# One normalisation of three moved from VectorE to GpSimd, with the steps around it reordered, in a softmax attention and mish feed-forward kernel

## The chip, the cores and the metric

The kernel runs on one core of a Trainium2 chip. The metric is the device time of one execution in microseconds (us); lower is better. Times are medians over several executions; one further execution was taken with the hardware profiler, and every duration below comes from it. Engines are called as the profile calls them: PE is TensorE (PEld its weight loads), DVE is VectorE, ACT is ScalarE, POOL is GpSimd, SP is SyncE, which here only issues DMAs.

## The reference

Attention over 8 batches, 12 heads, 448 positions and head size 64, then a feed-forward layer with mish over the 3584 rows (768 to 2048 to 768):

```python
scores = scale * np.matmul(q, k.transpose(0, 1, 3, 2))
m = np.max(scores, axis=-1, keepdims=True)
e = np.exp(scores - m)
attn = e / (np.sum(e, axis=-1, keepdims=True) + np.exp(-m) + 1e-09)
out = np.matmul(attn, v)
...
h = x @ w_in
g = h * np.tanh(log1p(exp(h)))        # mish
y = g @ w_out
```

## The kernel before

**Pairs and units.** Two heads of one batch form a pair; there are 48 pairs (0 to 47). Six head pairs make a batch. Pairs 0 to 5 are handled one by one in a head loop. From pair 6 on, three pairs form a unit; the loop variable `u` runs from 2 to 17, and units 2 to 15 hold attention (pairs `3u` to `3u+2`, the first of them is `p0`). Units are called u2, u3 and so on here. All instructions of an engine run in the order in which the program writes them (`tc.manual_schedule()`), so the place of a call in this loop is the place of its instructions in the queue of each engine.

**The exp stage of a unit** has twelve steps `n` (four steps for each pair, `s = n % 4`). A step lets ACT take the exponentials of one score tile (`exps`, L282; the row sums come with it), empties late PSUM tiles through DVE (`flush_late`), puts in filler matmuls of the second feed-forward product (`mm2_part`, L428, from u4 on), and issues the next scores on PE (L248 or L254), whose row maxima DVE takes (`negm`, L269). There are three score tiles `sc0` to `sc2`. In the steps with `s == 0` (n = 0, 4 and 8) the unit loads a pair that is four ahead (`load_pair`, three DMAs on SP, L120) and casts a pair that is three ahead to bf16 (`cast_pair`, three casts on POOL, L161 to L163). POOL also issues the weight loads (`load_w`, L147) in u2 to u4.

**The feed-forward stage of a unit** then runs eight steps `f`. Each is one column block of the first product (`mm1_mish`: six matmuls, L373, and one Mish on ACT, L379). At `f == 0` DVE computes the denominators (L295, L299) and normalises the first pair: `normalise` is seven multiplications in place, one for each tile of 128 rows, on `en` (L305), and then one transposing DMA on SP that makes `eT` from `en` (L312). At f = 1, 3 and 5 PE turns q and k of one pair of the next unit (`transpose_pair`, L178, into two banks of `sc2` and `sc1`), DVE copies the turned q out with the scale (`evac_qk`, L209, two instructions; L199 up to pair 11) and ACT copies k (L217). The copies are called q1, q2 and q3 here, the turnings t1, t2 and t3. At f = 1 and 3 the second and the third pair are normalised, behind q1 and q2 in DVE's queue. The score of the next unit's step 0 is issued at f = 3, those of steps 1 and 2 at f = 6 and 7.

**Attention times v** (`av_pair`, L349) of the unit's pairs runs in the exp stage of the unit after it; from u4 on in front of the last score of each pair (`av_with`). u2 and u3 follow the table `AV_AT` instead. Pairs 5, 6 and 7 (`BY_PE`) are not turned by a DMA but by PE (`turn_on_pe`, L323, copied out by DVE, L327); in u3 that is pair 6 at n = 0 (two pieces), 2 and 3, and pair 7 at n = 4 to 7. The exponentials of pairs 10 and 11 reuse the `en` buffers of pairs 6 and 7, so they can start only when these turnings have read them.

Of the kernel before, what the change touches and what calls it, by code (L numbers as in the profile page):

```python
# [9 lines left out]
FP32 = mybir.dt.float32  # L10
BF16 = mybir.dt.bfloat16
AF = mybir.ActivationFunctionType
ALU = mybir.AluOpType
# [6 lines left out]
def kernel(  # L20
# [9 lines left out]
    nc = tc.nc  # L30
# [10 lines left out]
    NTILE = 2 * S // 128  # L41
# [3 lines left out]
    FF_U = FF_T // UNITS_PER_B  # L45
# [17 lines left out]
    st_pool = pool("st", 5)  # L63
# [38 lines left out]
    def flush_late():  # L102
        while late:
            late.popleft()()
# [8 lines left out]
    def load_pair(p):  # L113
        if p >= N_PAIRS:
            return
        b, h0 = p // HP, (p % HP) * 2
        tiles = []
        for nm, src in (("q", q), ("k", k), ("v", v)):
            t = ld_pool.tile([SP_, 2, NT * D], FP32, tag=f"{nm}_f", name=f"{nm}_f")
            nc.sync.dma_start(  # L120
                out=t, in_=src[b, h0 : h0 + 2].rearrange("h (p t) d -> p h (t d)", t=NT)
            )
            tiles.append(t)
        loaded[p] = tiles
# [25 lines left out]
    def cast_pair(p):  # L150
        if p >= N_PAIRS:
            return
        q_f, k_f, v_f = loaded.pop(p)
        q_bf = bf_pool.tile([SP_, NT, 2, D], BF16, tag="q_bf", name="q_bf")
        k_bf = bf_pool.tile([SP_, NT, 2, D], BF16, tag="k_bf", name="k_bf")
        v_bf = bf_pool.tile([SP_, 2, NT * D], BF16, tag="v_bf", name="v_bf", bufs=12)
        by_t = "p h (t d) -> p t h d"
        cast_q, cast_k = nc.gpsimd.tensor_copy, nc.gpsimd.tensor_copy
        if p == 0:
            cast_q, cast_k = nc.vector.tensor_copy, nc.scalar.copy  # L160
        cast_q(out=q_bf, in_=q_f.rearrange(by_t, t=NT))  # L161
        cast_k(out=k_bf, in_=k_f.rearrange(by_t, t=NT))  # L162
        nc.gpsimd.tensor_copy(out=v_bf, in_=v_f)  # L163
        casted[p] = (q_bf, k_bf, v_bf)
# [56 lines left out]
    def scores_ahead(limit):  # L221

        while rg["next"] < limit and rg["used"] < len(sc_tiles):
            rg["used"] += 1
            scores(rg["next"])
            rg["next"] += 1
# [71 lines left out]
        )  # L298
        nc.vector.reciprocal(out=st["rden"], in_=st["den"])  # L299

    def normalise(p, dma=True):
        st = att[p]
        en = st["en"]
        for i in range(NTILE):
            nc.vector.tensor_scalar(  # L305
                out=en[:, :, i, 0:SP_], in0=en[:, :, i, 0:SP_],
                scalar1=st["rden"][:, i : i + 1], scalar2=None, op0=ALU.mult,
            )
        eT = eT_pool.tile([128, NT, 2 * S], BF16, tag="eT", name="eT")
        st["eT"] = eT  # L310
        if dma:
            nc.sync.dma_start_transpose(  # L312
                out=eT.rearrange("c j (i q) -> c (j i) q", q=128),
                in_=en.rearrange("q j i c -> q (j i c)"),
            )
# [19 lines left out]
    def av_pair(p, act=False, bank=None):  # L335
        b, hp = p // HP, p % HP
        eT = att[p]["eT"]
        v_bf = casted[p][2]
        if b not in xT:
            xT[b] = xT_pool.tile([128, DM_T, S], BF16, tag="xT", name="xT")  # L340
        av = mo_take() if bank is None else bank
        for j in range(NT):
            for h in range(2):
                if p >= DIAG_FROM:
                    by_h = eT[0:SP_, j, :].rearrange("c (i h r) -> c h i r", h=2, r=64)
                    e_h = by_h[:, h]
                else:
                    e_h = eT[0:SP_, j, h * S : (h + 1) * S]
                nc.tensor.matmul(  # L349
                    av[h * 64 : (h + 1) * 64, 0:S],  # L350
                    lhsT=v_bf[:, h, j * D : (j + 1) * D],
                    rhs=e_h,
                    start=(j == 0), stop=(j == NT - 1),
                )
        copy = nc.scalar.copy if act else nc.vector.tensor_copy

        def evac():
            copy(out=xT[b][:, hp, :], in_=av[:, 0:S])  # L358
            if bank is None:
                mo_free.append(av)  # L360

        late.append(evac)
        del att[p], casted[p], qkT[p]
# [77 lines left out]
    first_mm2 = 2 * UNITS_PER_B  # L441
# [24 lines left out]
    weight = [5.2] + [1.0] * (steps - STEPS) + [0.4] * (STEPS - 1)  # L466

    LEAD = UNIT_PAIRS + 1
    HEAD = HP

    BY_PE = {HEAD - 1: 1, HEAD: 0, HEAD + 1: STEPS}
    AV_AT = {0: {5: 3, 7: 4, 10: 5}, 1: {5: 6, 10: 7}}

    W_AT = ({5: 1, 9: 1}, {1: 1, 5: 1, 7: 1, 9: 1, 11: 1}, {1: 1, 3: 1, 5: 1, 7: 1})
    for p in range(UNIT_PAIRS):
# [10 lines left out]

    for p in range(HEAD):
        for s in range(STEPS):
# [7 lines left out]
            if s:  # L496
                flush_late()
            scores_ahead(HEAD * STEPS + 3)
            if s == (2 if p == HEAD - 1 else 0):
                load_pair(p + 4)  # L500
# [5 lines left out]
            if s == 1:  # L506
                if p:
                    normalise(p - 1)
            if s == 3 and p + 3 < HEAD + 2:
                transpose_pair(p + 3)  # L510
            if s == 3 and p >= 3:
                av_pair(p - 3, act=True)
    denominators(att[HEAD - 1])
    normalise(HEAD - 1, dma=HEAD - 1 not in BY_PE)

    for u in range(UNITS_PER_B, N_UNITS + 2 * UNITS_PER_B):
        attn = u < N_UNITS
        filler = deque()
        for part in plan.get(u, []):
            filler.extend(mm2_part(*part))  # L520
        total, done, acc = sum(w for _, w in filler), 0, 0.0
        p0 = u * UNIT_PAIRS
        if attn and u >= first_mm2:
            av_with.update({p0 + i: p0 + i - UNIT_PAIRS for i in range(UNIT_PAIRS)})
        end = min((u + 1) * UNIT_PAIRS, N_PAIRS) * STEPS

        for n in range(steps):
            pi, s = divmod(n, STEPS)
            p, idx = p0 + pi, p0 * STEPS + n
            late_tp = u == UNITS_PER_B and n == STEPS  # L530
            if late_tp:
                transpose_pair(p0 + 2)
            exps(idx)
            if late_tp:
                evac_qk(p0 + 2)
            if u == UNITS_PER_B + 1 and n == 0:
                av_pair(p0 - 1)
                for j in range(2):
                    turn_on_pe(HEAD, j)
            flush_late()  # L540
            acc += weight[n]
            want = int(total * acc / sum(weight) + 1e-6)
            while done < want:
                fn, w = filler.popleft()
                fn()
                done += w
            scores_ahead(end)
            if s == 0:
                load_pair(p + LEAD)
                cast_pair(p + LEAD - 1)  # L550
            early = AV_AT.get(u - UNITS_PER_B)
            if early is not None:
                if n in early:
                    av_pair(early[n])
                for pe, n0 in BY_PE.items():
                    first = 2 if pe == HEAD else 0
                    if pe // UNIT_PAIRS == u - 1 and n0 + first <= n < n0 + NT:
                        turn_on_pe(pe, n - n0)
            elif s == (2 if pi else 0) and N_PAIRS <= p < N_PAIRS + UNIT_PAIRS:
                av_pair(p - UNIT_PAIRS)  # L560
            if u - UNITS_PER_B < len(W_AT):
                load_w(W_AT[u - UNITS_PER_B].get(n, 0))
        assert done == total

        moe = u < N_UNITS + UNITS_PER_B
        b, w = (u - UNITS_PER_B) // UNITS_PER_B, u % UNITS_PER_B
        nxt = p0 + UNIT_PAIRS
        todo = sorted(range(p0, nxt), key=lambda p: p in BY_PE)
        for f in range(FF_U):
            if moe:  # L570
                mm1_mish(b, w * FF_U + f)
            if u == UNITS_PER_B and f in (2, 6) or u == UNITS_PER_B + 1 and f == 1:
                load_w(1)
            if not attn:
                continue
            if f == 0:
                denominators(att[p0]["whole"])
                normalise(todo[0], dma=todo[0] not in BY_PE)
            if f == 3:
                scores_ahead(min(nxt * STEPS + 1, N_PAIRS * STEPS))  # L580
            if f in (1, 3, 5):
                transpose_pair(nxt + f // 2, bank=f // 2 % 2)
                evac_qk(nxt + f // 2)
            if f in (1, 3):
                p = todo[(f + 1) // 2]
                normalise(p, dma=p not in BY_PE)
            if f >= FF_U - 2:
                scores_ahead(min(nxt * STEPS + f - FF_U + 4, N_PAIRS * STEPS))
    flush_late()
    assert not pieces and all(have == 4 for _, have in o_sbs.values())  # L590

# [29 lines left out]
```

## Time and profile before

| What | Value |
|---|---|
| Median of 3 runs | 510.11 us (509.66 to 511.9) |
| The profiled execution itself | 506.53 us |
| Its span from first to last instruction | 504.8 us, mean granted PE clock 0.986 |
| Busy in the span | PE 458.0, DVE 373.6, ACT 350.3, POOL 100.9 us |
| `en<-en,rden` on DVE (L305) | 336 instructions, 97.2 us |
| Casts on POOL (L161 to L163) | 142 instructions of about 623 ns |
| `eT<-en` transposing DMA (L312) | 45 issues, median 6.4 us from issue to landing |

The profiled execution took 506.53 us and lies 3.6 us under the median of the runs; 1.7 us of it are outside the span. In the trace's timeline a line gives start, duration, engine, line, operation, output and inputs, the number of instructions merged, and in square brackets the idle time before it and what ended that. The unit boundary used below is the one small exponential at the end of a unit's exp stage (L292): 98.46 us for u3, 126.87 for u4, then 153.74, 182.20, 210.26, 238.18 (u8), 265.97, 293.60, 321.53, 349.10, 376.73, 404.30 and 431.18 (u15).

### The profile page before, as it was taken

How to read it: one execution, taken by the hardware profiler on the slowest of the kernel's cores; microseconds unless marked ns; L12 is line 12 of the kernel's file. 1: busy time of each engine (PE TensorE's matmuls, PEld its weight loads, DVE VectorE, ACT ScalarE, POOL GpSimd, SP SyncE). 2: the span in 40 equal slices, each digit the busy share in tenths (PEclk: the TensorE clock that was granted, in tenths of full speed). 3: DMA queues.
4: the chain of work that ended last, by engine and by line, in shares of the span. 5: the costliest groups of instructions: out<-in, count | busy, mean ns of one | idle time of the engine just before them, and what ended most of it. 6: DMA issues, size and time to landing. Idle time of an engine off the chain costs nothing.

```text
span 504.8 us, 9065 instructions
## 1 busy us (share of the span) xinstructions
PE 458.0 (91%) x3120; PEld 250.5 (50%) x3120; DVE 373.6 (74%) x778; ACT 350.3 (69%) x906; POOL 100.9 (20%) x168
## 2 busy tenths in 40 slices
PE   4466987988999999999999999999999999999996
PEld 2122444544555555455555555555555555555573
DVE  4897997888979797978889797978798897530011
ACT  5988657768797877968696878879697879602300
POOL 4523263405022130402121120404040200000000
PEclk9999987899999999999999999999999999999999
DMA  8999999999998969698998879797989776670122
GB/s 227 189 200 242 250 196 241 197 179 251 153 252 192 188 169 214 199 202 217 188 250 167 192 148 226 200 215 203 203 233 182 184 131 145 120 171 11 53 53 73
DMA packets 209454, 92.21 MB, mean 183 GB/s; under 512 B 166272, under 2 KB 205952, under 8 KB 209408
## 3 DMA queue, kind: packets, MB, share of 16 engines
q1 hardware_dynamic: 201920, 85.35, 77.9%
q0 software_dynamic: 7488, 6.29, 8.5%
q8 instruction: 24, 0.39, 0.3%
q14 instruction: 22, 0.18, 0.1%
HBM read 45.61 MB, written 11.01 MB: 112 GB/s over the span
## 4 chain that ended last, share of the span: by engine, by line
PE 47%; DVE 31%; ACT 12%; DMA 5%; issue 3%; SPq 1%; POOL 0%; DVEq 0%; ACTq 0%; POOLq 0%
PE mo L428 20%; DVE en L305 12%; PE mo L373 11%; ACT en L282 11%; DVE negm L269 11%; PE sc L248 6%; PE sc L349 5%; DVE qd L209 3%; DMA k_f<-in_k_dram 3%; DMA eT<-en 2%; DVE xT L358 2%; PE sc L178 1%; PE mo L349 1%; PE sc L254 1%; PE mo L323 1%
## 5 line engine op out<-in xcount | busy, mean ns | idle before, releaser
L282 ACT ACTIVATE en<-sc,negm 128x448 bf16<-128x448 f32 x336 | 209.2, 636 | 30.5 <-DVE negm L269 15.4
L269 DVE TENSOR_REDUCE negm<-sc 128x2 f32<-128x896 f32 x192 | 181.5, 969 | 44.2 <-PE sc L248 33.3
L428 PE MATMUL mo<-w_out_sb,gT 128*128 128x384 bf16 (+2 forms) x1152 | 167.1, 309 | 0.0
L373 PE MATMUL mo<-xT,w_in_sb 128*128 128x448 bf16 x672 | 141.5, 355 | 0.4 <-DVE xT L358 0.3
L428 PEld LDWEIGHTS <-gT 128*128 128x128 bf16 (+1 forms) x1152 | 97.3, 100 | 56.5 <-issue 5.9
L379 ACT ACTIVATE gT<-mo 128x448 bf16<-128x448 f32 x112 | 59.3, 543 | 74.7 <-PE mo L373 74.5
L373 PEld LDWEIGHTS <-w_in_sb 128*128 128x128 bf16 x768 | 73.2, 98 | 64.4 <-issue 4.4
L305 DVE TENSOR_SCALAR en<-en,rden 128x448 bf16<-128x448 bf16 x336 | 97.2, 361 | 1.4
L161 POOL CAST q_bf<-q_f 112x512 bf16<-112x512 f32 x47 | 29.3, 623 | 282.9 <-DMA q_f<-in_q_dram 245.7
L414 DVE COPY o_sb<-mo 128x384 f32<-128x384 f32 (+1 forms) x64 | 32.1, 501 | 58.3 <-PE mo L428 58.1
L248 PE MATMUL sc<-kT,qd 128*128 128x448 bf16 x252 | 71.7, 354 | 3.6 <-DVE qd L209 2.7
L282 ACT ACTIVATION_READ_ACCUMULATOR en<-sc,negm 128x1 f32 x336 | 69.2, 206 | 0.0
L248 PEld LDWEIGHTS <-qd 128*128 128x128 bf16 x252 | 23.3, 97 | 35.9 <-issue 16.5
L349 PE MATMUL sc<-eT,v_bf 112*64 112x448 bf16 x288 | 34.0, 356 | 2.3 <-ACT en L282 1.8
L254 PE MATMUL sc<-kT,qd 64*128 64x448 bf16 x36 | 17.9, 515 | 18.1 <-ACT en L282 15.2
L349 PEld LDWEIGHTS <-v_bf 112*64 112x64 bf16 x384 | 21.3, 114 | 24.9 <-issue 17.0
L217 ACT COPY kT<-sc 128x448 bf16<-128x448 bf16 x39 | 20.8, 535 | 17.4 <-PE sc L178 17.4
L163 POOL CAST v_bf<-v_f 112x512 bf16<-112x512 f32 x48 | 29.9, 622 | 13.7 <-DMA v_f<-in_v_dram 12.8
L162 POOL CAST k_bf<-k_f 112x512 bf16<-112x512 f32 x47 | 29.3, 623 | 6.3 <-DMA k_f<-in_k_dram 4.5
L209 DVE TENSOR_SCALAR qd<-sc 64x448 bf16<-64x448 bf16 x72 | 27.8, 386 | 0.9
L178 PEld LDWEIGHTS <-q_bf 112*128 112x128 bf16 x192 | 14.4, 104 | 25.3 <-issue 11.8
L358 DVE CAST xT<-sc 128x448 bf16<-128x448 f32 x36 | 22.1, 614 | 0.0
(45 smaller groups left out, 251.3 us busy)
## 6 DMA issues: line engine op xcount, KB each, us to landing
q_f<-in_q_dram SPq DMA_DIRECT2D x48, 224.0 KB, 4.6
k_f<-in_k_dram SPq DMA_DIRECT2D x48, 224.0 KB, 4.8
v_f<-in_v_dram SPq DMA_DIRECT2D x48, 224.0 KB, 4.8
w_in_sb<-in_moe_w_in_dram POOLq DMA_DIRECT2D x12, 256.0 KB, 5.2
w_out_sb<-in_moe_w_out_dram POOLq DMA_DIRECT2D x8, 384.0 KB, 7.8
out_dram<-o_sb SPq DMA_DIRECT2D x7, 336.0 KB, 3.0
out_dram<-o_sb SPq DMA_DIRECT2D x8, 288.0 KB, 3.8
out_dram<-o_sb SPq DMA_DIRECT2D x8, 240.0 KB, 2.8
```

What stands on the lines that cost most here:

```text
L163: nc.gpsimd.tensor_copy(out=v_bf, in_=v_f)
L209: nc.vector.tensor_scalar(out=qd[rows, :, h, :], in0=q_ps[rows, 0:S].rearrange("d (i r) -> d i r", i=QB), scalar1=SCALE, scalar2=None, op0 ...
L248: nc.tensor.matmul(sc[:, bk, 0:S], lhsT=qT[:, i].rearrange("d h r -> d (h r)"), rhs=kT, start=True, stop=True,)
L269: nc.vector.tensor_reduce(out=negm, in_=sc[:, 0 : len(cols), 0:S], axis=AX.X, op=ALU.max, negate=True)
L282: nc.scalar.activation(out=st["en"][:, :, c, 0:SP_], in_=sc[:, bk, 0:S].rearrange("q (j c) -> q j c", j=NT), func=AF.Exp, bias=st["negm"][ ...
L305: nc.vector.tensor_scalar(out=en[:, :, i, 0:SP_], in0=en[:, :, i, 0:SP_], scalar1=st["rden"][:, i : i + 1], scalar2=None, op0=ALU.mult,)
L349: nc.tensor.matmul(av[h * 64 : (h + 1) * 64, 0:S], lhsT=v_bf[:, h, j * D : (j + 1) * D], rhs=e_h, start=(j == 0), stop=(j == NT - 1),)
L358: copy(out=xT[b][:, hp, :], in_=av[:, 0:S])
L373: nc.tensor.matmul(h_ps[:, 0:S], lhsT=w_in_sb[:, dm, ff * 128 : (ff + 1) * 128], rhs=xT[b][:, dm, :], start=(dm == 0), stop=(dm == DM_T - 1),)
L379: nc.scalar.activation(out=gT[b][:, ff, :], in_=h_ps[:, 0:S], func=AF.Mish)
L414: nc.vector.tensor_copy(out=o_sb[:, cols], in_=st["o"][:, 0:n_cols])
L428: nc.tensor.matmul(st["o"][r : r + n, 0:n_cols], lhsT=gT[bb][:, ff, c0 : c0 + n], rhs=w_out_sb[:, ff, cols], start=(ff == 0), stop=(ff == ...
```

## The change

From u4 on, the third pair of a unit is normalised by POOL instead of DVE: seven multiplications in the form with two scalars (the second is 1.0), placed at f = 4. Its reciprocals are first copied on DVE into a tile of their own (`rden2`). The second pair's normalisation moves on DVE from behind q1 (f = 1) to behind q2 (f = 3, after the score that is issued there and its maxima). In u2 and u3 the third one stays on DVE and moves to f = 7, behind the maxima of the scores issued there. Loads and casts come at exp steps n = 0, 3 and 6 (the first, fourth and seventh step) instead of 0, 4 and 8. In u3 the product of pair 8 no longer leads step 0 but comes at n = 3, in front of the turning of that step, and that of pair 6 moves from n = 5 to n = 6. The weight loads keep their steps, so some of them now stand behind a cast that they stood before.

```diff
-    def normalise(p, dma=True):
+    def normalise(p, dma=True, on_pool=False):
         st = att[p]
         en = st["en"]
+        if on_pool:
+            st["rden2"] = st_pool.tile([128, NTILE], FP32, tag="rden2", name="rden2")
+            nc.vector.tensor_copy(out=st["rden2"], in_=st["rden"])
         for i in range(NTILE):
-            nc.vector.tensor_scalar(
+            args = dict(
                 out=en[:, :, i, 0:SP_], in0=en[:, :, i, 0:SP_],
-                scalar1=st["rden"][:, i : i + 1], scalar2=None, op0=ALU.mult,
-            )
+                scalar1=st["rden2" if on_pool else "rden"][:, i : i + 1],
+            )
+            if on_pool:
+                nc.gpsimd.tensor_scalar(scalar2=1.0, op0=ALU.mult, op1=ALU.mult, **args)
+            else:
+                nc.vector.tensor_scalar(scalar2=None, op0=ALU.mult, **args)
...
+    LOAD_AT = (0, 3, 6)
...
-    AV_AT = {0: {5: 3, 7: 4, 10: 5}, 1: {5: 6, 10: 7}}
+    AV_AT = {0: {5: 3, 7: 4, 10: 5}, 1: {3: 8, 6: 6, 10: 7}}
...
             if u == UNITS_PER_B + 1 and n == 0:
-                av_pair(p0 - 1)
                 for j in range(2):
                     turn_on_pe(HEAD, j)
...
-            if s == 0:
-                load_pair(p + LEAD)
-                cast_pair(p + LEAD - 1)
+            if n in LOAD_AT:
+                load_pair(p0 + LOAD_AT.index(n) + LEAD)
+                cast_pair(p0 + LOAD_AT.index(n) + LEAD - 1)
...
-            if f in (1, 3):
-                p = todo[(f + 1) // 2]
-                normalise(p, dma=p not in BY_PE)
             if f >= FF_U - 2:
                 scores_ahead(min(nxt * STEPS + f - FF_U + 4, N_PAIRS * STEPS))
+            if f == 3:
+                normalise(todo[1], dma=todo[1] not in BY_PE)
+            if f == (4 if u >= first_mm2 else FF_U - 1):
+                normalise(todo[2], dma=todo[2] not in BY_PE, on_pool=u >= first_mm2)
```

## The prediction

> **What bounds the kernel now.** I read the page first (busy shares, then the chain that ended last), then the windows by unit, then the list of waits, then the timelines of single queues.
>
> ```profile
> PE 458.0 (91%) x3120; PEld 250.5 (50%) x3120; DVE 373.6 (74%) x778; ACT 350.3 (69%) x906; POOL 100.9 (20%) x168
> PE 47%; DVE 31%; ACT 12%; DMA 5%; issue 3%; SPq 1%; POOL 0%; DVEq 0%; ACTq 0%; POOLq 0%
> ```
>
> PE leads, yet a third of the chain runs through DVE. The windows cut at the unit boundaries say how much of that is real. Columns: window, length, then busy time of PE, PEld, DVE, ACT, POOL, granted clock, DMA share.
>
> ```profile
> 238.20:266.00 27.80, 26.70 (x183) 14.96 (x182) 23.35 (x48) 22.03 (x58) 6.41 (x11) 1.00 1.01 214
> 376.70:404.30 27.60, 27.24 (x214) 15.06 (x213) 22.80 (x48) 21.96 (x59) 3.88 (x7) 1.00 0.82 179
> ```
>
> From u4 on PE is idle for about 1 us in each 27 us. So DVE work that leaves is worth only the PE idle time that it ends. The list of waits says what ended it (total, times, longest):
>
> ```profile
> PE sc L178 <- DVE qd L209: 6.5, 12, 1.1
> PE sc L248 <- DVE qd L209: 2.7, 5, 0.8
> ```
>
> Nearly all of it waits for a q copy on DVE, at two places: t3 waits for q2 (L178), and the score at f = 3 waits for q1 (L248). In u8's feed-forward stage, DVE first, then PE, POOL, SP, and last PE in the next exp stage:
>
> ```profile
> 240.69 0.79 DVE L209 TENSOR_SCALAR qd<-sc 64x448 bf16<-64x448 bf16 x2
> 241.51 2.72 DVE L305 TENSOR_SCALAR en<-en,rden 128x448 bf16<-128x448 bf16 x7
> 244.27 1.09 DVE L269 TENSOR_REDUCE negm<-sc 128x2 f32<-128x896 f32 x1
> 245.28 0.78 DVE L209 TENSOR_SCALAR qd<-sc 64x448 bf16<-64x448 bf16 x2
> 246.09 1.81 DVE L305 TENSOR_SCALAR en<-en,rden 128x448 bf16<-128x448 bf16 x7
> ...
> 242.58 2.44 PE L373 MATMUL mo<-xT,w_in_sb 128*128 128x448 bf16 x12
> 246.11 0.36 PE L178 MATMUL sc<-ident,q_bf 112*128 112x112 bf16 x4 [1.10 <-DVE qd L209]
> ...
> 241.32 0.61 POOL L161 CAST q_bf<-q_f 112x512 bf16<-112x512 f32 x1 [4.21 <-DMA q_f<-in_q_dram]
> 241.88 0.65 POOL L162 CAST k_bf<-k_f 112x512 bf16<-112x512 f32 x1
> 242.48 0.65 POOL L163 CAST v_bf<-v_f 112x512 bf16<-112x512 f32 x1
> ...
> 240.84 13.49 SPq L312 DMA_TRANSPOSE eT<-en  x3
> 254.43 0.54 SPq L120 DMA_DIRECT2D q_f<-in_q_dram  x1
> ...
> 262.75 0.95 PE L349 MATMUL sc<-eT,v_bf 112*64 112x448 bf16 x8
> ```
>
> The second normalisation stands between q1 and q2, so q2 ends at 246.06 and t3, ready at 245.0, starts at 246.11. Three POOL casts ran beside that normalisation, which took 2.72 us; without casts it takes 1.81. Where casts fall on the first one instead (u5, u6, u7, u10, u11: 2.52 to 2.87 us), q1 is late and the score at f = 3 waits.
>
> **The idle time to be had.** t3 waits in u4 to u14 (us): 0.35, 0.44, 0.44, 0.45, 1.10, 0.31, 0.44, 0.44, 0.94, 0.25, 0.19, together 5.35. The score at f = 3 waits in u5, u6, u7, u10, u11: 0.53, 0.75, 0.66, 0.63, 0.30, together 2.87. In u3 t3 waits 1.11.
>
> **Second normalisation behind q2.** I retime u8. The score at f = 3 runs at 241.80 as before, its maxima then take DVE from 242.2 to 243.25, q2 to 244.05. PE comes to t3 at 245.0: no wait. The 5.35 and u3's 1.11 go. In u3 the q1 wait at f = 3 (0.49) stays; there two small memsets stand in front of q1. What is late next: normalisation two runs 244.05 to 245.87, so its transposing DMA starts at 245.9. SP was not free before about 245.65 anyhow (each issue holds it some 4.2 us), so 0.25 us.
>
> **Third normalisation on POOL.** DVE loses 7 x 0.26 = 1.81 us in twelve units and gains one copy of 128x7, bounded by the nearest row, the 0.18 us of the 128x21 denominators, and by nothing. It ends at about 246.05. q3 needs t3 (245.4) and DVE, so 246.05 to 246.85; the score that needs it is issued behind f = 7 at 248.06. The slack of 1.2 us covers the copy: cost nothing.
>
> No row shows the multiplication on POOL. Below, it cannot beat DVE's 0.26 us by any row; nearest is POOL's own cast of 512 elements, which starts every 0.56 us in a row, so 0.49 for 448; above I take two such casts at 0.61 each, 1.22, since the form has two multiplications. I take 0.55 (a little over the cast's rate): seven are 3.9 us, 246.05 to 249.9. SP is free for the third transposing DMA at 250.1. So POOL's slower work hides behind SP's queue. Behind this DMA on SP stand the loads of the next unit, and behind POOL's wait for the reciprocals stand the next casts, which PE needs some 20 us later. The third product ran on PE at 262.75 and would run at 261.65; the DMA lands 6.4 us after its issue, at 256.5. Slack 5.1 us, so POOL could take 0.55 + 5.1/7 = 1.28 us each before PE waits. At 1.22 the product is still covered, but the loads come 4.6 us later. POOL's seven run beside q3 and maxima that read PSUM; at 257.9 to 260.2 three casts ran beside such maxima, which kept their 1.04 us each. So I charge DVE nothing.
>
> GpSimd is the wrong place for this by one rule: the Trainium skill, GPSIMD Engine Reference, Engine selection, gives elementwise work to VectorE and calls GpSimd about two times slower for two inputs (near line rate for one). Prorating its two-input 4497 ns for 2048 gives an estimate of 0.98 us each: the third DMA would start 2.8 us later, which the slack above hides, and the sum could lose the 2.87 us of rival one. No run here shows POOL at this work yet.
>
> **Loads and casts at 0, 3 and 6.** SP issues them once the three transposing DMAs are out (254.43 in u8). The second load stood behind a store that waits for DVE (256.88 before 257.80); now it is ahead of that store in several units. The last casts before the boundary ended at 266.87, in the first normalisation's time; with the loads some 1.5 to 3 us earlier, and the pair behind them held back by POOL's normalisation, they end ahead of it. So the casts leave DVE's normalisations alone, and the 2.87 goes. The weight pieces that now stand behind a cast in u4 are issued by about 126 and land 7.8 us later, ahead of u5's use at 139: nothing.
>
> **The turnings in u3.** The product of pair 8 waited 1.5 us for its DMA at 80.70. Without it the first two turnings start at 79.2, but ACT's table load holds the first exponentials until 80.8 and DVE is now in the moved third normalisation until about 82, so the maxima come hardly earlier. At n = 3 that product stands in front of the last turning of pair 6, for which ACT already waited 1.60 us (86.94). It costs 0.95 us at full clock or 1.7 at the 0.50 granted in 84 to 92 us. I charge 1.2; were the clock full there, the stage would gain up to 3.
>
> **Last unit.** The three normalisations ran back to back (431.96, 5.25 us). The third DMA started at about 442.4, when SP was free; POOL would be done at 439.5. Nothing.
>
> **Sum.** 506.53 - 5.35 - 2.87 - 1.11 + 1.2 = 498.4 for the profiled execution, 8.1 less. Taken from the median 510.11: **502.0 us**.
>
> **Rivals.** *Casts stay late.* POOL at 1 to 1.2 us each, so loads and casts still meet the first normalisation, and the 2.87 stays: 504.9. For it: POOL has twelve times 7 new instructions in front of casts. Against: 8 us between the last loads and the boundary.
>
> *The wait is handed on.* PE runs into another queue as soon as it stops waiting: DMA, whose share is 1.01 in u8's window, or ACT, 22 us busy of 27. Then a unit stays near 27.7 and nothing moves: 510. Against: the same unit work needs only a 0.82 share in the window from 376.70, and units with little stall (0.19 in u14) do run at 26.9.
>
> *POOL too slow.* At 2.0 us each the seven end at 260.05, the third DMA lands at 266.5, and the product, due at 261.65, holds PE 4.8 us in each of eleven units: +53 on the 502, with the late casts' 2.9, about 558. It decides from about 1.35 us each, where the waits eat the whole gain. For it: no row of POOL reads a scalar per partition or does two operations. Against: 2.0 is over three times its cast.
>
> **Numbers.** Forecast 0.60, late casts 0.12, handed on 0.10, POOL too slow 0.18. A change of 0.5% (2.55 us) is about what a measurement can tell. Faster 0.72 (the first two), same 0.10, slower 0.18. Range: low is the sum with u3's 3 us gained instead of 1.2 lost, and a little, 497.5; high is the handed-on case with its small scatter, 511. Only slow POOL lies outside.
>
> **What would show it.** Right: t3 and the f = 3 score without waits on `qd`, PE idle per unit under 0.3 us, first normalisations all at 1.81, POOL's seven in 3.5 to 5 us, the third DMA starting as soon as SP is free. Wrong: PE waits for `eT` in front of the third product (slow POOL); casts still beside L305 (late casts); units of 27.7 with a new releaser (handed on).

## The result, and the profile after

The changed kernel takes 495.96 us (median of 4 runs, 494.59 to 496.47). The kernel before, run beside it, takes 510.46 us (4 runs, 509.66 to 511.9). The ratio is 0.9709 with a 95% interval of 0.9679 to 0.9739: 14.5 us less, where 8.1 were forecast, and 1.5 us below the range's low end.

The profiled execution after took 496.47 us (span 494.7, granted clock 0.989). It is 10.06 us shorter than the profiled execution before. So the two profiles differ by less than the two medians; this matters below.

The page after, busy times and then the shares of the chain that ended last:

```profile
PE 453.2 (92%) x3120; PEld 249.9 (51%) x3120; DVE 349.8 (71%) x706; ACT 349.1 (71%) x906; POOL 151.1 (31%) x252
PE 72%; DVE 12%; ACT 10%; issue 2%; DMA 1%; SPq 1%; POOL 0%; DVEq 0%; ACTq 0%; POOLq 0%
```

DVE's share of the chain fell from 31% to 12%, PE's rose from 47% to 72%, and POOL, half as busy again as before, has none of it. The windows show the same. First the kernel before from u4's boundary to u15's, then the kernel after: the same stretch, then one unit's length from the boundaries of u6 and of u8 (columns: window, length, busy time of PE, PEld, DVE, ACT, POOL, granted clock, DMA share, GB/s):

```profile
126.87:431.18 304.31, 295.57 (x2089) 164.27 (x2087) 254.52 (x528) 241.68 (x619) 53.11 (x87) 1.00 0.89 193
```

```profile
126.57:421.52 294.95, 293.40 (x2089) 164.45 (x2087) 231.76 (x462) 240.75 (x619) 102.12 (x170) 1.00 0.97 203
181.50:208.00 26.50, 26.50 (x183) 14.91 (x182) 20.80 (x42) 21.90 (x58) 8.89 (x15) 1.00 0.89 197
234.58:261.11 26.53, 26.53 (x183) 14.93 (x182) 20.93 (x42) 21.92 (x58) 9.79 (x17) 1.00 1.05 220
```

PE's idle time in eleven units falls from 8.74 to 1.55 us, and in the two single units there is none. The list of waits of PE in that stretch after (total, times, longest) has no t3 (L178) left:

```profile
PE sc L248 <- DVE qd L209: 0.7, 2, 0.4
PE mo L381 <- DVE o_sb L422: 0.4, 1, 0.4
```

In the changed code the normalisation is L316 on DVE and L314 on POOL, the copy of the reciprocals L307, the transposing DMA L320, the product with v L357, the first feed-forward product L381. u8's feed-forward stage after, by engine (DVE, PE, POOL, SP, and last the third product):

```profile
237.22 0.78 DVE L209 TENSOR_SCALAR qd<-sc 64x448 bf16<-64x448 bf16 x2
238.78 1.09 DVE L269 TENSOR_REDUCE negm<-sc 128x2 f32<-128x896 f32 x1 [0.78 <-PE sc L248]
239.79 0.78 DVE L209 TENSOR_SCALAR qd<-sc 64x448 bf16<-64x448 bf16 x2
240.60 1.81 DVE L316 TENSOR_SCALAR en<-en,rden 128x448 bf16<-128x448 bf16 x7
242.33 0.16 DVE L307 COPY rden<-rden 128x7 f32<-128x7 f32 x1
242.52 0.79 DVE L209 TENSOR_SCALAR qd<-sc 64x448 bf16<-64x448 bf16 x2
...
238.97 2.43 PE L381 MATMUL mo<-xT,w_in_sb 128*128 128x448 bf16 x12
241.24 0.36 PE L178 MATMUL sc<-ident,q_bf 112*128 112x112 bf16 x4
...
242.66 4.32 POOL L314 TENSOR_SCALAR en<-en,rden 128x448 bf16<-128x448 bf16 x7 [6.96 <-DVE rden L307]
246.92 0.61 POOL L161 CAST q_bf<-q_f 112x512 bf16<-112x512 f32 x1
...
237.71 13.74 SPq L320 DMA_TRANSPOSE eT<-en  x3
...
257.89 0.95 PE L357 MATMUL sc<-eT,v_bf 112*64 112x448 bf16 x8
```

q2 ends at 240.57, before t3 is due at 241.24. POOL's seven multiplications end at 246.98 and the third transposing DMA ends its issue at 251.45, so PE's third product at 257.89 waits for nothing. Behind POOL's seven stand casts of the next unit: that row turns out to matter most.

Lengths in us between unit boundaries (those of the small exponential, L292) put the gain in place. "Before again" is the first experiment below, the same code profiled once more. The first stretch, "u2 and u3" from here on, holds the feed-forward stages of u2 and u3, each with the exp stage behind it; the second holds those of u4 to u14, "the eleven units".

| Stretch | before | before again | after |
|---|---|---|---|
| u2's boundary to u4's | 61.56 | 64.80 | 60.85 |
| u4's boundary to u15's | 304.31 | 304.94 | 294.95 |
| u15's boundary to the end | 73.62 | 73.57 | 73.18 |

### The profile page after: what moved, and what is told of

The parts are those of the page before. It is cut to its first block, busy times and chain, and to the rows that moved or that the text cites. A ratio compares the mean times of both kernels' runs of the same rounds, so it can differ in the third digit from the quotient of the medians.

```text
span 494.7 us, 9027 instructions
## 1 busy us (share of the span) xinstructions
PE 453.2 (92%) x3120; PEld 249.9 (51%) x3120; DVE 349.8 (71%) x706; ACT 349.1 (71%) x906; POOL 151.1 (31%) x252
## 4 chain that ended last, share of the span: by engine, by line
PE 72%; DVE 12%; ACT 10%; issue 2%; DMA 1%; SPq 1%; POOL 0%; DVEq 0%; ACTq 0%; POOLq 0%
PE mo L436 24%; PE mo L381 24%; ACT en L282 9%; PE sc L248 8%; DVE negm L269 6%; PE sc L357 6%; DVE en L316 3%; PE sc L381 3%; PE sc L178 3%; PE mo L357 2%; DMA k_f<-in_k_dram 1%; PE sc L254 1%; DVE xT L366 1%; PE mo L331 1%; SPq L120 1%
## 5 line engine op out<-in xcount | busy, mean ns | idle before, releaser
L381 PE MATMUL mo<-xT,w_in_sb 128*128 128x448 bf16 x672 | 139.8, 352 | 1.3 <-DVE xT L366 1.0
L381 PEld LDWEIGHTS <-w_in_sb 128*128 128x128 bf16 x768 | 72.8, 98 | 64.6 <-issue 3.7
L314 POOL TENSOR_SCALAR en<-en,rden 128x448 bf16<-128x448 bf16 x84 | 51.8, 637 | 103.4 <-DVE rden L307 69.6
L316 DVE TENSOR_SCALAR en<-en,rden 128x448 bf16<-128x448 bf16 x252 | 69.8, 348 | 0.9
L357 PE MATMUL sc<-eT,v_bf 112*64 112x448 bf16 x288 | 34.0, 356 | 2.3 <-ACT en L282 1.8
L357 PEld LDWEIGHTS <-v_bf 112*64 112x64 bf16 x384 | 21.3, 115 | 22.8 <-issue 16.8
L178 PEld LDWEIGHTS <-q_bf 112*128 112x128 bf16 x192 | 14.4, 104 | 16.5 <-DVE q_bf L161 4.2
```

The lines of the kernel that those rows point to most:

```text
L178: nc.tensor.transpose(by_s[s][:, t * SP_ : (t + 1) * SP_], src[:, t].rearrange("p h d -> p (h d)"), ident[:SP_, :SP_],)
L314: nc.gpsimd.tensor_scalar(scalar2=1.0, op0=ALU.mult, op1=ALU.mult, **args)
L316: nc.vector.tensor_scalar(scalar2=None, op0=ALU.mult, **args)
L357: nc.tensor.matmul(av[h * 64 : (h + 1) * 64, 0:S], lhsT=v_bf[:, h, j * D : (j + 1) * D], rhs=e_h, start=(j == 0), stop=(j == NT - 1),)
L381: nc.tensor.matmul(h_ps[:, 0:S], lhsT=w_in_sb[:, dm, ff * 128 : (ff + 1) * 128], rhs=xT[b][:, dm, :], start=(dm == 0), stop=(dm == DM_T - 1),)
```

## The experiments

Two theories at first: A, the eleven units gain more than the profile before let one see; B, they gain what the profiles show, and the rest lies in u2 and u3, where the profiled execution before was luckier than the usual one. A third (C) was that the profiled execution is the short one of every kernel. All kernels compute the whole reference. "Before" is the kernel before on the same chip. Lines of the diffs are against the kernel after, unless it says "before".

### Which execution is the usual one

**e0_before_again**: no edit, the kernel before. **e11_changed_again**: no edit, the changed kernel.

> The kernel before, unchanged, for more executions and a second profiled one. The profiled pair of executions differs by 10.1 us (506.53 to 496.47), the medians by 14.5. Theory A (casts): the profiled execution of before was a lucky one; in the usual one more casts of POOL fall on the multiplications of DVE, so the waits of PE on the q copies in u4 to u15 are 11 to 13 us instead of 8 to 9, and the stretch from the boundary 126.87 to 431.18 is some 3 us longer than 304.3. Theory B (elsewhere): that stretch stays within 1 us of 304.3 and the 3 to 4 us lie in the head, u2 and u3 or the tail, where the clock of PE is reduced in some stages. Theory C: the profiler's execution is shorter for every kernel; then the new profiled execution is again near 506.5 while the timed runs are near 510.

> The changed kernel itself, unchanged, to stand beside the others on the same chip: 494.5 to 497. If the difference of the medians (14.5 us) holds against the difference of the two first profiled executions (10.1 us), the ratio to before is again 0.968 to 0.974 and the second profiled execution near 496 as the first.

e0: 511.21 us (12 runs, 507.45 to 512.54), ratio 1.0015 [0.9983, 1.0048]; its profiled execution took 510.79, 4.3 us more than the one shown before. e11: 495.76, ratio 0.9716 [0.9679, 0.9753]; profiled 496.13. That ends C. The eleven units in e0 take 304.94, 0.6 more than in the first profile; u2 and u3 take 64.80, 3.2 more. So B holds, as far as two profiles tell. One wait differs by more than this: the product of pair 8 at the head of u3's exp stage, which waits for its DMA. In e0's timeline, PE, then SP's issue of that DMA, then POOL's weight issues beside it:

```profile
85.38 1.71 PE L349 MATMUL mo<-eT,v_bf 112*64 112x448 bf16 x8 [5.63 <-DMA eT<-en]
...
71.72 9.51 SPq L312 DMA_TRANSPOSE eT<-en  x1
...
65.58 0.72 POOL L147 DMA_DIRECT2D w_in_sb<-in_moe_w_in_dram  x1
68.33 2.14 POOL L147 DMA_DIRECT2D w_in_sb<-in_moe_w_in_dram  x3
72.24 0.72 POOL L147 DMA_DIRECT2D w_in_sb<-in_moe_w_in_dram  x1
```

It waited 1.50 us in the profile that the prediction read, 5.63 here, and 6.00 and 8.18 in two kernels below that keep this order. The issue held SP 7.51 us there and the DMA landed 9.5 us after the issue began; here the two are 9.51 and 13.6. The first profile isn't outside the scatter of the runs, though: of 80 executions of the kernel before that ran beside the experiments (504.49 to 513.65 us), eleven took less than 507. The three runs that the prediction had (509.66 to 511.9) showed too little of it.

### What POOL's part brings

**e1_third_on_dve**: the third normalisation at the same place, f = 4, but on DVE.

```diff
-                normalise(todo[2], dma=todo[2] not in BY_PE, on_pool=u >= first_mm2)
+                normalise(todo[2], dma=todo[2] not in BY_PE)
```

> The changed kernel with the third normalisation back on DVE at the same place (f = 4), no copy of the reciprocals. The order behind q2, the loads at 0, 3 and 6 and the turnings first stay. If the order is what pays: t3 still does not wait; DVE has 1.81 us more in front of q3, which ends at about 1.8 us later and makes the score behind f = 7 wait 0.4 to 0.6 us in each of eleven units, so 4 to 6 us slower than the changed kernel, about 500 to 502. If relief of DVE is what pays: 8 us or more slower, 504 and up.

509.6 us, 0.9984 [0.9954, 1.0013]: the whole gain is gone. By its number this is the second expectation, that relief of DVE is what pays; the rows say otherwise. In e1's list of waits in the eleven units:

```profile
PE sc L248 <- DVE qd L209: 10.5, 17, 1.0
```

In front of q3 the normalisation makes the score behind f = 7 wait, 0.56 us in each unit. The other six, 4.4 us, are waits for q1 at f = 3, which I had taken to be ended by the new load steps. That called for two more kernels.

**e3_dve_behind_q3**: on DVE at f = 5, behind q3. **e9_gate_only**: as e3, and at f = 4 POOL does one small copy that must wait for DVE, and no multiplication.

```diff
 e3
-            if f == (4 if u >= first_mm2 else FF_U - 1):
-                normalise(todo[2], dma=todo[2] not in BY_PE, on_pool=u >= first_mm2)
+            if f == (5 if u >= first_mm2 else FF_U - 1):
+                normalise(todo[2], dma=todo[2] not in BY_PE)
 e9, as e3 and
+            if f == 4 and u >= first_mm2:
+                rden2 = st_pool.tile([128, NTILE], FP32, tag="rden2", name="rden2")
+                nc.vector.tensor_copy(out=rden2, in_=att[todo[2]]["rden"])
+                gate = st_pool.tile([128, NTILE], FP32, tag="gate", name="gate")
+                nc.gpsimd.tensor_copy(out=gate, in_=rden2)
```

> As e1_third_on_dve, but the third normalisation stands on DVE at f = 5, behind q3. Then no q copy waits for it, and SP is not free for its transposing DMA before that anyhow. If only the place in DVE's queue matters, GpSimd is not needed: within 1.5 us of the changed kernel, 495 to 498. If DVE's load itself matters (the maxima behind it come late for the first exponentials): 2 us or more slower than the changed kernel.

> As e3_dve_behind_q3 (all three normalisations on DVE, the third behind q3; 503.2 us), but POOL gets one small copy of the reciprocals where the changed kernel has its seven multiplications. It does no work, but in POOL's queue it holds the next unit's first casts back until DVE is through with the second normalisation. If holding the casts back is what POOL's part gives: the waits at f = 3 (3.98 us together in e3_dve_behind_q3) go and the time is that of the changed kernel, 495.5 to 498. If it is the 1.81 us less on DVE in each unit: still 501 to 504.

e3: 503.24 us, 0.9872 [0.9821, 0.9923]. t3 waits no more, the score at f = 3 still does (five times in the eleven units, 2.8 us; two waits of a score for ACT make 1.2 more). Its u9 boundary, DVE, POOL and PE:

```profile
265.15 2.52 DVE L316 TENSOR_SCALAR en<-en,rden 128x448 bf16<-128x448 bf16 x7
...
264.69 0.61 POOL L161 CAST q_bf<-q_f 112x512 bf16<-112x512 f32 x1 [0.24 <-DMA q_f<-in_q_dram]
265.33 0.64 POOL L162 CAST k_bf<-k_f 112x512 bf16<-112x512 f32 x1
265.91 0.65 POOL L163 CAST v_bf<-v_f 112x512 bf16<-112x512 f32 x1
...
268.43 0.55 PE L248 MATMUL sc<-kT,qd 128*128 128x448 bf16 x2 [0.30 <-DVE qd L209]
```

POOL, with nothing in its queue that waits, goes straight on to casts of the next unit as their loads land, and these fall on DVE's first normalisation. e9: 497.1 us, 0.9743 [0.9707, 0.978]. The same place in e9:

```profile
263.48 1.81 DVE L316 TENSOR_SCALAR en<-en,rden 128x448 bf16<-128x448 bf16 x7
...
270.65 0.19 POOL L600 COPY gate<-rden 128x7 f32<-128x7 f32 x1 [7.97 <-DVE rden L598]
270.78 0.61 POOL L161 CAST q_bf<-q_f 112x512 bf16<-112x512 f32 x1
```

Here the small copy holds those casts back, the normalisation is back at 1.81 us, and 6.1 of the 7.3 us between the medians of e3 and the changed kernel are there, with all normalisations on DVE. In the profiles the eleven units take 298.91 us in e3, 295.03 in e9 and 294.95 in the changed kernel, so in this stretch the gate gives all but 0.1 of it. So it is chiefly the wait in POOL's queue that counts, not the work taken from DVE.

**e5_pool_double**: every tile is multiplied on POOL a second time, by 1.0.

```diff
+    ones = singles.tile([128, 1], FP32)
+    nc.vector.memset(ones, 1.0)
...
+                nc.gpsimd.tensor_scalar(scalar2=1.0, op0=ALU.mult, op1=ALU.mult, **args)
+                args.update(scalar1=ones[:, 0:1])
```

> The changed kernel with POOL's work doubled: each of the seven multiplications of a unit is followed by one more by 1.0, 14 instructions of 0.62 us, 8.7 instead of 4.3 us. The prediction put the limit at 1.28 us per tile (now 1.24) before the third product waits for its DMA: then that product still does not wait, or by less than 0.5 us, and the cost is loads that start 4 us later and casts that meet the first normalisation again: 1 to 6 us slower, 497 to 502. If the covered time is shorter than worked out: PE waits for eT in each unit, 10 us or more slower.

509.88 us, 1.0028 [0.9991, 1.0066]: 13.9 us over the changed kernel. Lines of e5 on PE, the first for late casts, the second for the late DMA:

```profile
298.39 0.55 PE L250 MATMUL sc<-kT,qd 128*128 128x448 bf16 x2 [1.04 <-DVE qd L211]
346.73 0.95 PE L361 MATMUL sc<-eT,v_bf 112*64 112x448 bf16 x8 [1.46 <-DMA eT<-en]
```

Fourteen instructions took 9.38 us in u8 (247.52 to 256.90), 1.34 per tile. Waits for `eT` sum to 3.9 us in the eleven units (seven of them), waits for q1 at f = 3 to 4.5; one more wait of 2.0, for ACT, stands in a unit of 30.90 us whose granted clock was 0.94. Neither expectation fits: the waits for `eT` are as small as the first one had it, but the loss is as large as in the second. In the profile the eleven units are 12.0 us longer than in the changed kernel, of which these three kinds of wait are 10.4.

### What the load steps bring

**e2_loads_only** (before): loads and casts at 0, 3, 6. **e4_old_load_steps**: the changed kernel with them at 0, 4, 8.

```diff
 e2 (before)
+    LOAD_AT = (0, 3, 6)
...
-            if s == 0:
-                load_pair(p + LEAD)
-                cast_pair(p + LEAD - 1)
+            if n in LOAD_AT:
+                load_pair(p0 + LOAD_AT.index(n) + LEAD)
+                cast_pair(p0 + LOAD_AT.index(n) + LEAD - 1)
 e4
-    LOAD_AT = (0, 3, 6)
+    LOAD_AT = (0, 4, 8)
```

> The kernel before with one part of the change: loads and casts at exp steps 0, 3 and 6. If casts that fall on DVE's multiplications are the cause of the waits at f = 3 and of the long t3 waits: the first normalisations are all near 1.81 us and the waits at f = 3 (2.87 us in the profile of before) are gone, t3 still waits 0.2 to 0.4 us per unit: 3 to 5 us faster than before, 505 to 507. If the loads only move the casts without freeing DVE: within 1 us of before.

> The changed kernel with loads and casts back at exp steps 0, 4 and 8; the rest of the change stays. If the earlier loads are what keeps the casts off DVE's multiplications: the waits at f = 3 come back in about half of the units (2 to 5 us in the stretch of u4 to u15), 498 to 501. If POOL's seven multiplications, which stand in front of the next cast in POOL's queue, already hold the casts back: under 1 us, 495 to 497.

e2: 509.34 us, 0.9989 [0.9947, 1.0031]. e4: 495.45, 0.9735 [0.9688, 0.9782], not distinguishable from the changed kernel. With POOL's part in place the load steps bring nothing. Without it they bring nothing that the medians can tell, and 2.7 us at most by the interval; in e2's profile the long waits of t3 are gone (none over 0.4 us, where the kernel before has 1.1), but casts still fall on the first normalisation in about half of the units and the score at f = 3 still waits. The list of waits of e2 in the eleven units has both waits, and e4's POOL shows why it has neither:

```profile
PE sc L178 <- DVE qd L209: 4.0, 11, 0.4
PE sc L248 <- DVE qd L209: 2.0, 5, 0.7
```

```profile
241.67 4.32 POOL L314 TENSOR_SCALAR en<-en,rden 128x448 bf16<-128x448 bf16 x7 [6.88 <-DVE rden L307]
245.93 0.61 POOL L161 CAST q_bf<-q_f 112x512 bf16<-112x512 f32 x1
```

### What the order in u3 brings

**e8_turnings_only** (before): u3's order alone. **e7_product_first_again**: the changed kernel without it. **e6_products_behind_turnings**: all three products behind the turnings.

```diff
 e8 (before), undone in e7
-    AV_AT = {0: {5: 3, 7: 4, 10: 5}, 1: {5: 6, 10: 7}}
+    AV_AT = {0: {5: 3, 7: 4, 10: 5}, 1: {3: 8, 6: 6, 10: 7}}
...
-                av_pair(p0 - 1)
 e6
+    AV_AT = {0: {5: 3, 7: 4, 10: 5}, 1: {8: 8, 9: 6, 10: 7}}
```

> The kernel before with only the order of u3 changed: turnings lead step 0, the product of pair 8 at n = 3 and that of pair 6 at n = 6. If the wait for the DMA of pair 8 (5.63 us in the second profiled execution of before) is what this edit takes away, as its undoing on the changed kernel (3.3 us slower) says: 2.5 to 4.5 us faster than before, 506 to 508, and a narrower scatter. If its gain exists only together with the rest of the change: within 1 us of before.

> The changed kernel with the order of u3 undone: the product of pair 8 leads step 0 again, that of pair 6 at n = 5. In three profiled executions with the old order PE waited 1.50, 5.63 and 8.18 us there for the DMA of pair 8. If the extra gain over the prediction comes from this wait, which the profile shown with the kernel before had caught at its shortest: 3 to 5 us slower than the changed kernel, 499 to 501, and a wider scatter. If the prediction's price for this edit (1.2 us lost by it) was right: about 1 us faster, 495.

> The changed kernel, but in u3 the products of pairs 8 and 6 come behind all turnings (n = 8 and 9 instead of 3 and 6). In the changed kernel ACT waits 3.36 and 3.21 us for the last turning of pairs 6 and 7, with one product of 1.7 us in front of each. If these products are on that path: both waits shrink by 1 to 1.7 us, 2 to 3 us faster than the changed kernel, 493 to 494. If the turnings are late for their own reasons (copies of DVE, the clock): within 0.7 us.

e8: 508.91 us, 0.9957 [0.9931, 0.9983], 2.2 us less than before, a little under what was expected. e7: 499.24, 0.9801 [0.976, 0.9841], 3.3 us more than the changed kernel. The product of pair 8 in e7, in e8, in the changed kernel and in e11, the changed kernel again:

```profile
84.22 1.71 PE L357 MATMUL mo<-eT,v_bf 112*64 112x448 bf16 x8 [6.00 <-DMA eT<-en]
```

```profile
87.25 1.71 PE L349 MATMUL mo<-eT,v_bf 112*64 112x448 bf16 x8 [1.43 <-DMA eT<-en]
```

```profile
85.45 1.70 PE L357 MATMUL mo<-eT,v_bf 112*64 112x448 bf16 x8
```

```profile
85.39 1.70 PE L357 MATMUL mo<-eT,v_bf 112*64 112x448 bf16 x8 [1.46 <-DMA eT<-en]
```

At n = 3 the DMA is there, or nearly; at the head of the stage PE stands still for it. In e8 SP's issue took 13.29 us, the longest seen, and in e11 12.05, so even n = 3 was 1.4 to 1.5 us too early there. The time isn't the wait alone: between u2's boundary and u3's e8 takes 34.07 us and e0 36.38, 2.3 less, as the medians; PE waits 4.2 us less for the DMA and 2.6 more for ACT's exponentials. In e7's one profile this stretch is 34.42, only 0.8 to 1.1 longer than in the two profiles of the changed kernel (33.67 and 33.35); where the rest of its 3.3 us lies isn't shown. e6: 496.52, 0.9749 [0.9703, 0.9794]: ACT's waits shrink from 3.36 and 3.21 us to 1.73 and 2.12, but the three products then run as one lump of 3.86 us, and the time from u3's boundary to u4's grows to 29.5 us from 27.2. No gain.

### Where that wait comes from, and a faster version

**e12_weights_later** (before): the weight pieces that POOL issues in u2's feed-forward stage and at u3's n = 1 come at u3's n = 5. **e10_u2_behind_q1**: the changed kernel with u2's first normalisation behind q1 and pair 8's product at n = 4. **e13_weights_later_best**: e10 and e12's edit together.

```diff
 e12 (before), and e13
-    W_AT = ({5: 1, 9: 1}, {1: 1, 5: 1, 7: 1, 9: 1, 11: 1}, {1: 1, 3: 1, 5: 1, 7: 1})
+    W_AT = ({5: 1, 9: 1}, {5: 4, 7: 1, 9: 1, 11: 1}, {1: 1, 3: 1, 5: 1, 7: 1})
...
-            if u == UNITS_PER_B and f in (2, 6) or u == UNITS_PER_B + 1 and f == 1:
+            if u == UNITS_PER_B + 1 and f == 1:
 e10, and e13
-    AV_AT = {0: {5: 3, 7: 4, 10: 5}, 1: {3: 8, 6: 6, 10: 7}}
+    AV_AT = {0: {5: 3, 7: 4, 10: 5}, 1: {4: 8, 6: 6, 10: 7}}
...
-                normalise(todo[0], dma=todo[0] not in BY_PE)
+                if u != UNITS_PER_B:
+                    normalise(todo[0], dma=todo[0] not in BY_PE)
...
+            if f == 1 and u == UNITS_PER_B:
+                normalise(todo[0], dma=todo[0] not in BY_PE)
```

> The kernel before with four weight pieces issued later: the two of u2's feed-forward stage and the one of u3's n = 1 go to u3's n = 5 (four there). POOL then starts one weight transfer instead of three at about 67 us and none at 71, just ahead of and beside the transposing DMA of pair 8 (on SP at 71 us, held there 7.5 to 13.3 us in the profiles). If these transfers are what delays that DMA: PE's wait for it in u3 falls from 5.6 us to under 2, the first normalisation of u2 is shorter too, 3 to 6 us faster than before, 505 to 508. If the loads of pairs or the transposing DMA itself set its time: the wait stays at 4 us or more and the time within 1.5 us of before.

> The changed kernel with two more edits around u2 and u3: in u2 the first normalisation (pair 8) stands behind q1 on DVE instead of ahead of it, and the product of pair 8 comes one step later in u3 (n = 4, behind the last turning of pair 6). In u2 that normalisation is long (3.6 us and more beside casts and weight loads of POOL), q1 is late by it and PE waits 1.4 to 3.4 us at f = 3. If that wait is on the path: 1.5 to 3.5 us faster than the changed kernel, 492.5 to 494.5. If the delay of pair 8's DMA or of the second normalisation takes its place: within 0.7 us.

> The variant e10_u2_behind_q1 (494.2 us) with the same four weight pieces issued later. The product of pair 8 hardly waits there any more, so less is left: if POOL's weight loads still lengthen DVE's multiplications in u2, 0.5 to 2 us faster, 492 to 494; if nothing of them is on the path, 494 to 495; if the pieces now come too late for u3's feed-forward stage, slower by the wait.

e12: 505.24 us, 0.9927 [0.9899, 0.9954]: 4.8 us off the kernel before, by moving weight issues alone. From u2's boundary to u3's it takes 31.42 us, 5.0 less than e0. Its PE and SP:

```profile
76.39 0.95 PE L349 MATMUL mo<-eT,v_bf 112*64 112x448 bf16 x8
...
68.99 4.94 SPq L312 DMA_TRANSPOSE eT<-en  x1
```

The issue takes 4.94 us and the DMA lands 7.4 us after its start; PE waits for nothing there. In e13 the two are 4.98 and 6.5. In the fourteen profiles with the weight pieces in their old place the issue took 5.60 to 13.29 us and the landing 7.8 to 16.5. So the weight transfers are the likely cause of the long ones, and that isn't proved: the two kernels without them are at the low end, yet others come close to it with them (5.60 and 7.8 in e6). How they would do it (DMA engines, or descriptors on POOL) was not taken apart. Part of the gain is that the DMA starts earlier, since u2's first normalisation takes 2.28 us instead of 4.28, with fewer of POOL's issues beside it.

e10: 494.24, 0.9685 [0.9649, 0.9721], 1.5 us less than e11 on the same chip, though the two intervals overlap; u2 and u3 take 58.11 us against 60.85 after. e13: 493.77, 0.9683 [0.9647, 0.9719], the fastest seen, but its interval and e10's cover each other; once u3's order no longer waits for that DMA, quieting it brings nothing that these runs show.

## Why the prediction was right or wrong

**The idle time to be had: right, and priced a little too low.** t3's waits are gone, and those at f = 3 came down to two of 0.7 us together. (Of the 2.87 forecast there, the 0.63 of u10 stands in the trace as a wait for ACT.) PE's idle time fell by 7.2 us, with 8.22 forecast. The eleven units became 9.4 us shorter: PE's busy time fell by another 2.2 us at the same 2089 matmuls and the same granted clock of 1.00. This comes from the same waits. In the trace a matmul starts before the one in front of it has ended: in u8 after, the twelve of L381 end at 241.40 and t3 starts at 241.24; before, they ended at 245.02 and t3 started at 246.11. So each wait costs, beyond the idle time that the list gives, an overlap of 0.16 us. There are 16 waits in the eleven units before and 3 after, and 13 x 0.16 is 2.1 us. The wait of u3 shows the same: the stretch from u3's boundary to u4's became 1.23 us shorter (28.41 to 27.18), where 1.11 was forecast.

**Second normalisation behind q2: right.** As retimed: q2 ends ahead of t3, and nothing new is late but one wait of 0.4 us (L381 for `o_sb`).

**Third normalisation on POOL: right in size, wrong in what it is for.** 0.55 us each was forecast; the line's instructions measure 0.627 to 0.640, seven in 4.32 us, and SP's queue hides them, all but some 0.3 us at most: the third DMA's issue starts as POOL ends. The copy took 0.16 us. The maxima beside it kept 1.09 us, so charging DVE nothing held. By the rule of the Trainium skill (GPSIMD Engine Reference, Engine selection), one tensor input goes at about line rate on GpSimd and two at half the speed. The trace does not agree with the first: seven in 4.32 us stand against DVE's 1.81, 2.4 times; and the 0.98 prorated from the page was too long.

The price of a slower POOL held, as far as the waits for `eT` go. What the prediction had as the slack in front of the third product (1.28) fits e5's small waits for `eT`: at 1.34 they should be 0.42 us a unit, 4.6 together, and are 3.9. That e5 gave the time of the kernel before, as the prediction let POOL do from about 1.35 us each, is partly luck: the gain that it had to eat was 14.5 us and not 8.1, and e5 lost 13.9, of which the waits for `eT` and q1 are 8.4.

**Loads and casts at 0, 3 and 6: wrong cause.** It was credited with the 2.87 us. e2 shows that these steps leave the waits at f = 3 (2.0 us in five), and e4 that they bring nothing beside POOL's part. The 2.87 went all the same, because POOL's multiplications wait for reciprocals, and so hold the next unit's casts behind DVE's normalisations (e3 against e9). The prediction saw this ("the pair behind them held back by POOL's normalisation") and took it for a help to the load steps; it was nearly the whole of it.

**The turnings in u3: the step that failed.** It charged +1.2 us. e7 puts the edit at -3.3 on the changed kernel, e8 at -2.2 on the kernel before. The working rested on a wait of 1.5 us for pair 8's DMA, the value of one execution; in e0, e7 and e2, which keep the old order, it is 5.63, 6.00 and 8.18. On the execution that was read even the sign was right: the stretch from u2's boundary to u3's took 33.15 us before and 33.67 after. On the usual one it wasn't: from 36.38 (e0) it went to 33.35 (e11). With 5.6 in it, the same working would have had a gain. What the prediction named as a cost, the product at half clock in front of a turning, is there (1.70 us), and is less than the wait that it replaces.

**Sum, and taking it from the median: wrong by the same cause.** On the profiled execution the sum gave 498.4 and 496.47 was measured, 1.9 apart: 1.1 in the eleven units, 0.7 in u2's boundary to u3's, 0.1 in u3's t3. On the medians 502.0 stands against 495.96. The other 4.1 us come from carrying 8.1 over to a median that lay 3.6 us above the execution read. By e0's profile 3.2 us of such a distance lie in u2 and u3, where the wait for pair 8's DMA is 4.1 us longer, and there the change gains. The distance was stated and not asked after. The range's low end had the 3 us of u3 in it, and not the 1.4 more in the eleven units and the 0.8 at the two ends that follow here, so it stopped 1.5 us short. Against the usual execution (e0 to e11: 509.0 to 494.3 in span, 14.7 less) the gain is 9.6 in the eleven units (8.22 forecast), 1.2 from u3's boundary to u4's (1.11 forecast), 3.0 from u2's boundary to u3's, where 1.2 was to be lost, and 0.4 each ahead and behind. Of the 6.6 us between the 8.1 forecast and these 14.7, 4.2 lie in the stretch that the term of the turnings prices.

**The rivals.** Handed-on waits and a slow POOL did not come, and late casts are left in one unit only (u5, whose first normalisation takes 2.66 us); e3 shows the first of them, e5 the first and a mild form of the third.

## What to carry to other kernels

Before a wait for a DMA is priced, see how it differs between executions; where the profiled execution stands apart from the median, ask which wait that distance is, for the change may end it. An engine off the critical path runs ahead in its own queue and can fall on another engine at a bad moment: an instruction that waits there may be worth more than the work it does, so test the queue's order and the work apart (e3 and e9 here). Undo the parts of a change one by one: one edit credited with 2.9 us brought nothing that the runs could tell, and one charged with 1.2 brought 2 to 3.

## What the runs showed of the hardware

POOL's work lengthens DVE's multiplications in SBUF. Seven of them take DVE 1.81 us alone, 2.52 beside three casts (e3), 4.28, 4.72 and 5.54 beside POOL's casts and weight issues in u2 (before, e0 and e3). The longest single one in e3 took 2.19 us (69.03 to 71.22), against a median of 0.33; it ended 0.13 us after a cast that followed three weight issues on POOL. DVE's maxima, which read PSUM, kept 1.09 beside POOL. This agrees with the Trainium skill, SBUF — State Buffer, SBUF: two separate sides, which has the two engines share a port pair as an exclusive lock: of a VectorE instruction in a mode that uses both ports and a GpSimd instruction, the one that starts first shuts the other out.

A transposing DMA of one size held SP's queue 4.24 us at the median of the kernel before, and that of pair 8 from 4.94 to 13.29 us over all kernels; it landed 6.5 to 16.5 us after its issue began. The length of the issue alone doesn't give the landing: in e7 an issue of 7.02 us landed after 12.3, in the profile before one of 7.51 after 9.5. In u3's exp stage of the changed kernel the granted clock was 0.50 from 84 to 88 us, with PE busy all the time; the eight matmuls of the product there take 1.70 us where they take 0.95 at full clock.
